# Attention over channels and a GELU layer in one kernel: the fifth chunk's squares of k folded, a copy of v moved to ScalarE, two fillers fewer, and a new order of steps up to block 6

## The chip, the cores and the metric

The kernel runs on one core of a Trainium2 chip. The metric is the time of one execution on the device in microseconds; here it is the median of three runs. A core has TensorE (matmuls, PE in the profile), VectorE (DVE), ScalarE (ACT), GpSimd (POOL), SyncE (SP) and 16 DMA engines. Each engine works through its own list in order.

## The reference

The inputs are q, k and v of shape (4, 6080, 256), w_in of (256, 2048) and w_out of (2048, 256), all in float32.

```python
qn = q / (np.linalg.norm(q, axis=1, keepdims=True) + 1e-06)
kn = k / (np.linalg.norm(k, axis=1, keepdims=True) + 1e-06)
s = kn.transpose(0, 2, 1) @ qn / tau            # 256 x 256 for each batch
a = np.exp(s - s.max(-1, keepdims=True))
a /= a.sum(-1, keepdims=True) + 1e-09
x = (v @ a).reshape(24320, 256)
h = x @ w_in
g = 0.5 * h * (1.0 + np.tanh(c * (h + 0.044715 * h * h * h)))   # c = sqrt(2 / pi)
out = g @ w_out
```

## The kernel before, in words

**Two halves for each batch.** For each of the four batches the kernel needs the Gram matrix G (q against k over 6080 rows) and the sums of squares of the columns of q and of k. From these come the scores and their exponentials (eT). Since v is only multiplied by a and then by w_in, the kernel builds aw, which is a times w_in (256 x 2048), once for each batch, and multiplies v's transposed rows (vT) by that. The rows of the output are worked in 25 blocks of about 1024 rows, each in two halves t=0 and t=1 of 512 rows. A block's first product is vT by aw with GELU on ScalarE, its second g by w_out. Parts of both go through seven instead of eight products of sub-blocks (lines 628 and 739), with the extra sums on VectorE.

**The first batch** cannot lie beside other blocks, so it is a stage of its own. Its rows come in six chunks (`FIRST`), 8 rows for each partition and 7 in the second. The first chunk is loaded in float32 and cast on chip; the others are cast by GpSimd's DMAs, the sixth in five pieces. For each chunk ScalarE squares q and VectorE squares k (line 172), side by side in one tile of 128 x 8 x 512. For the first four chunks `fold_first` (line 186) adds rows 0 to 3 and 4 to 7 of that tile, so that four rows are left. `gram_first` (line 199) does the Gram matmuls of a chunk. `ss_rows` sums squares over the partitions with matmuls against ones: for q one column at a time (line 217), for k one matmul of 256 columns for each row (line 223). On TensorE the sums of a chunk stand right ahead of the next chunk's Gram matmuls, and between the two `warm(n)` issues n matmuls of 256 columns whose result is not used (line 402). In the fifth and sixth chunk nothing is folded.

**From the sums to the first block.** Behind the last sums stand `warm(8)`, then `pe_vt(0, 0)`: TensorE's transposes of v's first half (line 337), then `scores` (lines 350 to 365: logarithms, exponentials and eT on ScalarE, S on VectorE), two copies of the transposed half out of PSUM on VectorE (`pe_vt_copy`, line 341), the load of the GELU table (line 886), and `first_aw`: row sums, their reciprocal rs (line 386) and the first 512 columns of aw, 256 of them copied by VectorE in four pieces (line 392) and 256 by ScalarE (line 395).

**The order of everything else** is a list written out by hand or by a planner beforehand (`ORDER`, 4017 steps), which the kernel walks through while it is built; the engines' lists follow it. A step is a block or batch and a short name:

- `0:j30` is the first product of block 0, 128 columns number 3, half 0 (line 560); `0:J30` its GELU (line 572).
- `0:s6m1` and the like are the products and sums of the seven-product scheme (lines 628 to 662).
- `b0:aw4` is a piece of aw for batch 0 on TensorE (line 501), `b0:ac4` its copy.
- `0:vp1` and `0:vc10` transpose a half of v on TensorE and copy it. Blocks 0 and 1 have three halves done so. The other halves are cast by a DMA of GpSimd (`1:lv1`, line 309) and transposed by a DMA of SyncE (`1:lt1`, line 321).
- `b1:lq0`, `b1:lk0` load a chunk of q or k of the next batch (line 246), `b1:r0.0` is a Gram row of it (line 296), `b1:zq0` its square on ScalarE, `b1:dk0` on VectorE, `b1:f0.1` a fold.
- `:pA11`, `:pF0` and others prepare the combinations of w_out.
- `0:T1a`, `0:M1A`, `0:c11`, `0:O0` are the sums, products, transposes and stores of the second half.

A load in the list waits for the matmul that stands last ahead of it (`GATE`). PSUM has eight accumulators, `FREE[1]`; one is taken from the front of the list and given back at its end.

**Buffers.** The pool `yout`, tag `ot`, has three buffers in rotation. In the first batch it holds the folded squares, then v's first halves as loaded for TensorE's transposes, later two tiles for w_out's sums and the output tiles:

```python
a1 = yout.tile([128, 4, 512], BF16, tag="ot", name=f"a1_{c}")
V0[m, t] = x = yout.tile([128, HALF // 128, C], BF16, tag="ot", name=f"v{m}_{t}")
```

Of the kernel before, what the change touches and what calls it, by code (L numbers as in the profile page):

```python
# [18 lines left out]
def kernel(  # L19
# [320 lines left out]
    def pe_vt_copy(m, t, cc):  # L340
        nc.vector.tensor_copy(vt(m)[:, t, cc, :], VPS[m, t][:, cc, :])
# [626 lines left out]
0:j01 0:j31 b0:w12 0:J80 0:s6ap 0:s6m7 0:s7m5 0:J61 :pA11 0:s6m3 0:J31 0:jb1 0:j41 b0:w01 0:J01
0:j90 0:ja0 :pF0 0:s6G1 0:s6ax 0:Jb1 0:s7y5 0:j71 0:M1A 0:Ja0 :pA12 b0:w03 0:J41 0:s6m4 0:J71 0:s7ap
:pF1 0:s6Gx 0:s7m7 b1:lk1 2:lv0 0:T3a 1:j50 0:M1B 0:J90 0:s7ax b1:lq2 0:s7m3 1:j01 b1:lk2 1:j10  # L970
0:s6Gr 1:J50 0:s7G1 b1:lk3 b1:r0.0 b1:r0.1 :pS2 0:s7m4 1:j51 1:j21 0:T1a 1:vs0 0:T2a 1:J01 1:j41
3:lv0 1:J10 0:x1 b1:dk0 b1:r0.2 b1:r0.3 8:lv0 b1:lq3 1:j31 1:J21 0:M2A 0:s7Gr 1:s3m1 b1:lk5 0:M2B
0:s7Gx b1:zq0 1:J31 :pS1 0:c11 0:T3b 0:M6A 1:s3cq b1:r1.0 1:j00 b1:r1.1 1:s3m5 1:vs1 1:J41 1:s3m2
0:T1b 1:J00 2:lv1 1:j11 b1:f0.1 0:M5A 1:J51 1:s3y5 b1:r1.2 1:s4m1 1:s3m6 1:s3ap 1:s3G0 b1:r1.3 1:j30
0:M5B 1:J11 b1:r2.0 :pNA 1:J30 1:s3m7 0:T2b 1:s4cq 4:lv0 1:s4m5 1:s4m2 0:y5 1:s4y5 1:s3m3 1:s3ax
1:vs2 1:s4m6 1:s4ap b1:zk1 1:s4G0 :pS4 b1:lq4 0:M6B 1:s3m4 b1:r2.1 1:s3G1 b1:r2.2 b1:r2.3 0:ap
b1:lk4 1:s5m5 b1:r3.0 1:s3Gx b1:zq1 1:s4m3 1:s4m7 1:j40 b1:r3.1 b1:lq5 1:s4ax 1:J40 0:M3A 1:s3Gr
b1:dk2 1:s4m4 b1:r3.2 1:s4G1 0:T4a 0:M3B b1:f1.1 1:s5m1 1:s6m1 1:s4Gx 1:s4Gr 1:s5cq 0:M7A 1:s5m2
1:s6cq 0:c12 1:s6m5 1:s5y5 1:s5G0 1:s5m6 0:T4b 0:M7B 1:s6m2 1:s6m6 1:j20 1:s6y5 1:s5ap 1:s5m7 2:lt1
b1:f1.2 b1:r3.3 1:s6ap b1:zq2 1:J20 b1:r4.0 1:s5ax 1:s6G0 b1:f2.1 1:s5m3 1:s6m3 2:lt0 1:s5G1 1:M1A  # L980
1:s7m1 1:s7m5 0:ax b1:r4.1 1:s6m7 1:s5m4 1:s5Gx 1:s6G1 b1:r4.2 1:s7y5 1:M1B 1:s7cq b1:zk3 1:s7m6
b1:f1.3 0:M4A 1:T3a 1:s5Gr 1:s6ax 1:s7ap 1:s6m4 1:s6Gx 1:s7m2 1:s7m7 b1:zq3 1:T1a 1:s7m3 b1:lk6
0:M4B 1:s7ax b1:f3.1 1:s6Gr 1:s7G0 b1:r4.3 1:s7G1 b1:lq6 2:j21 0:c21 2:j30 b1:lq7 b1:r5.0 1:x1 3:lv1
1:s7Gx 1:s7m4 2:J30 2:j20 2:j01 3:lt1 1:s7Gr 1:M2A b1:f3.2 2:j10 2:J21 2:J20 2:J01 2:s2m1 1:M2B
2:vs0 1:T3b 2:s2cq 2:J10 1:T1b 2:vs1 2:s2m5 2:j00 2:s2m6 2:s2y5 1:c11 2:vs2 2:s2m2 b1:dk4 2:s2ap
# [6 lines left out]
2:j31 2:s5m7 3:J31 2:s4Gx b1:dk6 2:s5ax 2:s6cq 2:s6y5 1:c22 1:O1 4:lv1 b1:lq8 b1:lk8 5:lv1 2:s5m3
2:J31 2:s5Gx 1:M4B 2:s6m2 2:s6m6 b1:r6.2 3:j21 b1:lk10 2:s5m4 1:c21 3:j10 b1:lq9 2:s6ap 2:s5G1
2:s7m1 3:J21 b1:r6.3 3:J10 2:s7cq 2:s6m3 2:T3a 2:s6m7 2:s7m5 b1:r7.0 2:s6G1 2:s6G0 b1:f5.2 b1:r7.1
2:s6ax b1:r7.2 2:s7m2 3:j11 2:s7m6 2:s6m4 2:s7y5 2:M1A 2:s5Gr 3:s2m1 3:J11 b1:f6.1 3:j01 2:s6Gx
2:s7ap 2:s6Gr 5:lv0 2:s7m7 b1:f5.3 2:s7m3 2:M1B 2:s7G0 3:j00 2:T1a 2:s7G1 b1:r7.3 2:s7ax 2:s7m4
3:J01 3:j20 2:x1 2:T2a 2:s7Gx 3:vs0 b1:zq7 b1:lq10 2:T3b 2:s7Gr 2:M2A 3:J00 3:J20 3:s2cq 2:M6A
b1:lq11 b1:f5.4 b1:lk9 b1:zk7 3:vs1 3:j30 2:M2B 3:s2m5 3:J30 3:s2m2 2:M5A 3:s2y5 2:T1b 2:c11 b1:lk11
2:M5B 2:T2b 3:s2G0 2:y5 3:s3m1 3:s2m6 b1:f7.1 3:s3cq 3:s2ap 3:vs2 2:M6B b1:zq9 3:s3m5 3:s3y5 2:ap
3:s3m6 3:s2m3 3:s2m7 b1:r8.0 3:s2G1 3:s3m2 2:M7A 3:s2ax 3:s2m4 2:M7B 3:s3ap b1:zq8 3:s4m1 3:s2Gr  # L1000
3:s3m3 3:s3G0 4:lt0 3:s4m5 b1:f7.2 b1:r8.1 2:M3A 3:s2Gx b1:r8.2 3:s4cq 3:s4m6 2:T4b 3:s4y5 2:ax 1:O0
2:T4a 3:s3G1 b1:zk9 3:s3m7 3:s4ap 3:s4m2 3:s4G0 3:s3ax 2:M3B 2:c12 3:s5m5 3:s3Gx 3:s4m7 3:s4m3 4:lt1
3:s3m4 b1:f7.3 3:s5m1 2:M4A 3:s4G1 2:M4B 3:s5cq 3:s3Gr 3:s5m2 3:s4ax 3:s6m1 3:s5m6 b1:dk8 3:s4Gx
b1:r8.3 b1:r9.0 3:s5y5 3:s5G0 2:c22 3:s6cq 3:s4m4 b1:r9.1 2:c21 5:lt0 3:s5ap 3:s6m5 3:s4Gr 3:s5m7
b1:f7.4 4:j30 3:s5m3 3:s6m2 3:s6y5 4:J30 b1:r9.2 b1:f8.1 3:s6G0 3:s7m1 b1:f9.1 3:s5ax b1:r9.3
b1:r10.0 b1:f9.2 3:s7cq 3:s6m6 3:s5G1 3:s7m5 2:O0 3:s7y5 b1:r10.1 b1:r10.2 3:s7m6 4:j00 b1:r10.3
3:s5Gx b1:r11.0 b1:zq11 b1:r11.1 3:s5m4 3:s6ap b1:r11.2 3:s7ap 3:s6m3 3:s7m7 3:s6m7 3:T3a 3:s5Gr
3:s7m3 5:lt1 3:s6ax 4:J00 3:s7m2 3:T1a 3:s7G1 4:j20 3:s6Gx 3:s6G1 4:j10 3:s7ax 3:s6m4 b1:dk10 3:s7G0
# [285 lines left out]
```

## Time and profile before

| what | value |
|---|---|
| median of three runs | 683.23 us (683.1 to 683.32) |
| the profiled execution | 683.62 us, its span 681.8 us |
| granted TensorE clock | 0.999 |
| busy: PE, DVE, ACT, POOL | 663.4, 626.1, 635.2, 87.8 us |
| bytes moved by DMA, mean rate | 78.80 MB, 116 GB/s |

Busy time is the time in which an engine had at least one instruction in work. Matmuls and ScalarE's steps overlap with their successors, so a step's duration is longer than its share: GELUs of 512 columns show a mean of 663 ns, and in a dense stretch (five in 2.55 us) follow each other at about 0.5 us. In the chain of waits a matmul of 512 columns has 0.215 us, and of 256 columns about 0.109. The time that an execution takes outside of its span is the difference of the first two figures in its row, 1.82 us.

### The profile page before, as it was taken

The numbers are of one execution on the slowest core, as the hardware profiler recorded it, in microseconds if no ns is written. First come the engines' busy times: TensorE is split into PE (matmuls) and PEld (weight loads), VectorE is DVE, ScalarE is ACT, GpSimd is POOL, SyncE is SP. The second block draws the span as 40 slices with busy tenths as digits, with TensorE's granted clock in tenths as the row PEclk, the third lists the DMA queues.
The fourth block names the chain that finished last, engine by engine and source line by source line (L and its number), as shares of the span: only waits on it lengthen the run. The fifth ranks groups of instructions, "written<-read, shape, count | busy, mean of one in ns | idle before, by whom it ended". The sixth has DMA issues, their size and how long they took to land.

```text
span 681.8 us, 10259 instructions
## 1 busy us (share of the span) xinstructions
PE 663.4 (97%) x3471; PEld 333.5 (49%) x3471; DVE 626.1 (92%) x922; ACT 635.2 (93%) x1224; POOL 87.8 (13%) x163
## 2 busy tenths in 40 slices
...
GB/s 241 208 258 157 122 139 163 140 87 129 79 137 81 136 163 131 141 68 120 115 136 43 158 98 147 126 117 78 62 68 106 75 67 122 39 55 78 83 31 121
DMA packets 165093, 78.80 MB, mean 116 GB/s; under 512 B 148992, under 2 KB 153472, under 8 KB 164320
## 3 DMA queue, kind: packets, MB, share of 16 engines
...
q10 hardware_dynamic: 1248, 1.28, 0.6%
q8 instruction: 27, 0.44, 0.3%
...
## 4 chain that ended last, share of the span: by engine, by line
PE 85%; DMA 6%; ACT 4%; DVE 3%; issue 1%; SPq 0%; POOL 0%; DVEq 0%; ACTq 0%; POOLq 0%
PE u L739 22%; PE rb L628 15%; PE j L560 13%; PE p L739 11%; PE qb L628 8%; PE c L739 5%; PE G L296 4%; PE qa L628 4%; DMA qk<-in_k_dram 3%; PE awp L501 2%; DMA out_dram<-ot 2%; DMA qk<-in_q_dram 1%; ACT sq L266 1%; ACT qa L643 1%; ACT g L572 1%
## 5 line engine op out<-in xcount | busy, mean ns | idle before, releaser
L739 PEld LDWEIGHTS <-wcomb 128*128 128x128 bf16 x1400 | 136.7, 98 | 146.2 <-issue 1.9
L739 PE MATMUL u<-t,wcomb 128*128 128x512 bf16 (+3 forms) x600 | 145.4, 368 | 0.0
L572 ACT ACTIVATE g<-j 128x512 bf16<-128x512 f32 (+1 forms) x204 | 127.0, 663 | 2.2 <-PE j L560 2.2
L560 PE MATMUL j<-vT,aw 128*128 128x512 bf16 (+2 forms) x456 | 126.6, 376 | 0.2 <-DVE aw L392 0.2
L648 DVE TENSOR_TENSOR qb<-rb,yw 128x512 f32<-128x512 f32 (+2 forms) x137 | 92.6, 680 | 9.9 <-PE rb L628 7.5
L628 PE MATMUL rb<-tv,sw 128*128 128x512 bf16 (+2 forms) x274 | 98.5, 374 | 0.0
L651 DVE TENSOR_TENSOR xw<-rb,yw 128x512 f32<-128x512 f32 (+2 forms) x137 | 91.8, 671 | 6.0 <-PE rb L628 3.5
L739 PE MATMUL p<-g,wcomb 128*128 128x512 bf16 (+3 forms) x400 | 96.4, 368 | 0.6 <-DVE g L712 0.5
L662 ACT ACTIVATE g<-xw 128x512 bf16<-128x512 f32 (+2 forms) x137 | 92.1, 675 | 1.3 <-DVE xw L651 1.3
L653 ACT ACTIVATE g<-qa 128x512 bf16<-128x512 f32 (+2 forms) x137 | 87.0, 640 | 2.8 <-PE qa L628 2.8
L656 ACT ACTIVATE g<-qb 128x512 bf16<-128x512 f32 (+2 forms) x137 | 87.6, 641 | 1.9 <-PE qb L628 1.6
L643 ACT ACTIVATE qa<-rb 128x512 f32<-128x512 f32 (+2 forms) x137 | 86.8, 638 | 1.7 <-PE rb L628 0.8
L646 ACT ACTIVATE yw<-qb 128x512 f32<-128x512 f32 (+2 forms) x137 | 87.1, 642 | 0.8 <-PE qb L628 0.5
L659 ACT ACTIVATE g<-rb 128x512 bf16<-128x512 f32 (+2 forms) x137 | 86.2, 640 | 1.4 <-PE rb L628 1.2
L628 PEld LDWEIGHTS <-sw 128*128 128x128 bf16 x548 | 53.6, 98 | 56.9 <-issue 1.9
L560 PEld LDWEIGHTS <-aw 128*128 128x128 bf16 x456 | 44.6, 98 | 45.2 <-DVE aw L392 0.7
L628 PEld LDWEIGHTS <-aw 128*128 128x128 bf16 x411 | 40.3, 98 | 42.3
L720 DVE TENSOR_TENSOR t<-g,g 128x2048 bf16<-128x2048 bf16 (+3 forms) x50 | 58.2, 1164 | 1.7 <-ACT g L662 0.8
L712 DVE TENSOR_TENSOR g<-g 128x2048 bf16<-128x2048 bf16 (+3 forms) x50 | 58.1, 1162 | 0.3
L718 DVE TENSOR_TENSOR t<-g,g 128x2048 bf16<-128x2048 bf16 (+3 forms) x50 | 57.8, 1160 | 0.1
L722 DVE TENSOR_TENSOR t<-t,g 128x2048 bf16<-128x2048 bf16 (+3 forms) x50 | 57.5, 1160 | 0.0
L309 POOL DMA_DIRECT2D vb<-in_v_dram x47 | 23.6, 503 | 222.1 <-PE rb L628 123.9
...
## 6 DMA issues: line engine op xcount, KB each, us to landing
...
wst<-in_moe_w_out_dram POOLq DMA_DIRECT2D x2, 1024.0 KB, 11.2
...
```

The source lines that it names most:

```text
L560: GATE[0] = nc.tensor.matmul(hp[:, :n].rearrange("p (t x) -> p t x", t=2) if t == 2 else hp[:, :n], lhsT=AW[b][:, cc, fc * 128 : fc * 128 ...
L572: nc.scalar.activation(g[:, t, fc % 8, :hc], hp[:, :hc], AF.Gelu_apprx_tanh)
L628: GATE[0] = nc.tensor.matmul(acc[:, :hc], lhsT=lhs, rhs=rhs, start=i in (1, 5), stop=True, skip_group_check=True)
L643: nc.scalar.activation(Q0[m, p][:, :hc], RB[m, p][:, :hc], AF.Copy)
L646: nc.scalar.activation(YW[m, p][:, :hc], Q1[m, p][:, :hc], AF.Copy)
L648: nc.vector.tensor_add(Q1[m, p][:, :hc], RB[m, p][:, :hc], YW[m, p][:, :hc])
L651: nc.vector.tensor_add(XW[m, p][:, :hc], RB[m, p][:, :hc], YW.pop((m, p))[:, :hc])
L653: nc.scalar.activation(g[:, 0, e, :hc], Q0.pop((m, p))[:, :hc], AF.Gelu_apprx_tanh)
L656: nc.scalar.activation(g[:, 1, e, :hc], Q1.pop((m, p))[:, :hc], AF.Gelu_apprx_tanh)
L659: nc.scalar.activation(g[:, 0, e + 1, :hc], RB.pop((m, p))[:, :hc], AF.Gelu_apprx_tanh)
L662: nc.scalar.activation(g[:, 1, e + 1, :hc], XW.pop((m, p))[:, :hc], AF.Gelu_apprx_tanh)
L739: GATE[0] = nc.tensor.matmul(ACCS[m, acc][:, :hc], lhsT=wcomb[:, w, fc, :], rhs=x[:, fc, :], start=first and k_ == 0, stop=k_ == 3, skip_g ...
```

## The change

In the first batch the squares of k of the fifth chunk (c = 4) are folded to four rows too, into a tile of the `ot` pool; the squares of q of that chunk stay as they are. `ss_rows` then takes four matmuls for k there instead of eight. Ahead of v's first transposes stand six fillers instead of eight. The second of the two copies of v's first transposed half is done by ScalarE. `square_later` can now take GpSimd as an engine, by steps `eq` and `ek`, but no step of the new list is one. The list `ORDER` holds the same 4017 steps; up to its 1099th, in block 6, they stand in another order, and behind that in the same.

```diff
+    SQK0 = {}
+
+    def fold_k(c):
+        a1 = yout.tile([128, 4, 512], BF16, tag="ot", name=f"a1_{c}")
+        nc.vector.tensor_add(a1[:, :, 256:512], SQ0[c][:, 0:4, 256:512], SQ0[c][:, 4:8, 256:512])
+        SQK0[c] = a1
...
     def ss_rows(c, which, rows=None):
         last = c == len(FIRST) - 1
-        n = N0.get(c, 8)
+        folded = which == 1 and c in SQK0
+        n = 4 if folded else N0.get(c, 8)
...
-        sq = SQ0[c]
+        sq = SQK0[c] if folded else SQ0[c]
...
     def pe_vt_copy(m, t, cc):
-        nc.vector.tensor_copy(vt(m)[:, t, cc, :], VPS[m, t][:, cc, :])
+        if (m, t, cc) == (0, 0, 1):
+            nc.scalar.copy(vt(m)[:, t, cc, :], VPS[m, t][:, cc, :])
+        else:
+            nc.vector.tensor_copy(vt(m)[:, t, cc, :], VPS[m, t][:, cc, :])
...
             if c < nch - 2:
                 fold_first(c)
+            else:
+                fold_k(c)
...
-        warm(8)
+        warm(6)
         pe_vt(0, 0)
         scores()
         pe_vt_copy(0, 0, 0)
```

The first steps of the list, before and after (cut):

```diff
-0:j00 b0:aw2 b0:aw3 0:j30 b0:ac2 0:J00 0:j10 b0:aw4 b0:ac3 b0:aw5 b0:aw6 0:J30 0:j20 0:J10 b1:lq1
-b0:w02 b0:w00 0:j60 b0:ac4 0:vp1 b0:ac6 0:s6m1 1:lv1 0:j40 0:J20 0:J60 b0:ac5 0:s7m1 0:s6cq 0:J40
...
+0:j00 0:j10 0:J10 b0:aw2 1:lv1 b0:aw3 b0:ac2 0:j20 b0:ac3 0:j30 b0:aw4 b0:w02 b0:aw5 b0:w00 0:j40
+0:J30 b0:ac4 b0:aw6 b0:ac5 0:j70 0:J20 1:lt1 0:vp1 b1:lq0 b0:ac6 0:vc10 0:J00 0:j80 0:J40 0:j60
+0:vc11 b0:w01 0:s6m1 0:J70 0:j90 0:vs0 0:J80 b0:aw7 0:jb1 0:s7m1 0:J60 0:s6cq b0:ac7 0:j81 0:vs1
+b1:lk0 0:j01 0:J90 b0:w10 0:Jb1 0:j11 0:s6m2 :pA11 0:s7cq 0:J81 0:J01 1:vp0 0:s7m2 b0:w12 b0:w03
+0:ja0 0:s6m5 b0:w11 1:vc00 0:J11 0:j51 0:s7G0 0:s6G0 0:j41 0:j21 0:s7m6 0:s6y5 0:vs2 0:J41 0:J51
...
```

More of the change, by code (lines that the diff above doesn't have):

```diff
@@ L251, with square_later @@
     SQ = {}
-    def square_later(b, c, which, on_act):
+    def square_later(b, c, which, on):
         n = chunk(c)[1]
@@ L968 @@
[L968 to L985, printed above, removed]
@@ L992 @@
[L992 to L1008, printed above, removed]
@@ L1019 @@
-4:s7G0 5:j01 4:s6G1 4:s7ap b1:krp 4:M1A 5:J01 4:s7m7 5:j00 b1:S0 5:j51 4:T3a 4:s5Gr 5:j50 4:s6Gx
-3:O1 b1:th0 4:s6m4 b1:S1 b1:th1 5:J00 4:s7ax 4:T1a b1:dn 4:s6Gr 5:j31 4:M1B b1:rc1 4:s7m4 4:s7m3
-5:J31 b1:rc3 b1:rc0 5:j41 b1:rc2 6:lt0 4:M5A 5:vs0 4:s7Gr 5:j21 5:J51 4:x1 5:j10 5:J50 4:s7G1 b1:eT
-5:J21 4:M2A 4:T2a 5:J41 5:s3m1 5:j30 5:s3cq 4:M2B b1:rsum 5:s3m2 5:J30 b1:aw6 5:J10 b1:rs 5:s3G0
-2:O1 4:s7Gx 5:vs1 b2:lq1 4:c11 5:j40 5:J40 b1:aw4 5:s3m5 4:M6A b1:ac6 5:s3m6 b1:aw2 5:s3y5 4:T3b
-b1:ac4 b1:aw3 5:vs2 5:s3ap b1:ac2 4:T1b b1:aw0 5:s3m3 5:s4m1 b1:aw7 b1:ac3 b1:w12 b1:ac0 5:s3m7
@@ new lines @@
+4:s6G0 4:s5Gx 3:c21 4:s5m4 b1:krp b1:S0 4:s5G1 b1:S1 4:s7m2 3:O1 4:T3a 4:s5Gr 4:s7G0 4:s6m7 4:s7m5
+5:j10 4:s6ax 5:j00 6:lt0 b1:th0 5:J10 4:M1A b1:th1 5:j51 4:s7y5 b1:dn 4:s7m6 4:T1a 4:M1B 4:s7ap
+5:J00 b1:rc2 4:s6Gx 4:s6m3 5:j30 4:s6m4 5:J51 4:s7m7 4:s6Gr 5:j50 4:s7ax 4:M5A 4:s7m4 5:J30 4:x1
+b1:rc3 b1:rc1 4:s7m3 4:s6G1 5:s3m1 4:s7Gr b1:rc0 5:J50 b1:eT 4:M2A 5:j01 5:j31 4:M2B 4:s7G1 5:vs0
+5:J01 b1:rsum 5:s3cq b1:aw6 5:J31 5:s3m2 5:vs1 b1:aw4 5:s3m6 b1:rs 4:s7Gx 5:j41 5:s3G0 5:s3m5 4:c11
+b2:lq1 b1:aw3 4:T2a b1:ac6 4:T3b b1:ac4 5:s3y5 5:j21 b1:aw2 5:J21 b1:w12 b1:ac2 5:s3ap 4:M6A b1:aw7
@@ new lines @@
+6:s5Gr 6:s6m7 6:s7G0 6:s7m5 6:s7y5 b2:r0.2 6:s6G1 7:j00 5:c22 6:s6ax 6:s7m6 b2:r0.3 6:j30 5:O1
+7:s2m1 b2:lq4 b2:r1.0 6:s7ap 10:lv0 6:s6Gx 6:J30 6:s7m3 6:s7m7 b2:lk5 6:s6m4 7:j11 6:s7G1 b2:r1.1
+7:s2cq b2:f2.1 6:s7ax 7:j10 7:J11 b2:f1.3 6:s7m4 b2:r1.2 6:s6Gr 6:s7Gr 7:s2m2 7:vs0 6:j00 7:j21
+b2:r1.3 9:lv0 7:vs1 7:s2m5 7:s2G0 b2:r2.0 b2:r2.1 6:J00 6:s7Gx 7:s3m1 7:s2y5 7:J21 6:T3a 6:T1a 7:J00
+b2:r2.2 6:M1A b2:r2.3 7:s2m6 7:s3cq 6:M1B 7:s3m2 b2:r3.0 b2:lq6 7:J10 6:x1 7:j31 7:s2ap 7:s2m3
+7:s3G0 b2:lq5 7:J31 7:s2m7 7:s3m6 7:s2G1 7:s3m5 7:vs2 6:M2A b2:lk4 7:s5m1 6:T3b 7:s2ax 6:T2a 7:s3y5
@@ new lines @@
+b2:r4.3 b2:r5.0 6:c22 7:s6m7 6:O1 b2:f3.4 7:s5Gr 7:s5Gx b2:lk7 b2:lq8 7:s7cq 7:s6m3 6:M4A 7:s6ax
+b2:r5.1 7:T3a 7:s7y5 b2:zk5 8:j00 7:s7m6 b2:lk8 9:lv1 7:s6G1 13:lv1 7:s6Gx 6:M4B 8:j11 7:s7ap 6:c21
+8:J00 7:s7m7 7:s6m4 7:s7m3 8:J11 8:j20 7:s7ax 7:s7m2 8:j30 7:s6Gr 7:s7m4 b2:r5.2 8:J20 8:j10 7:s7G0
+7:T1a 7:M1A 7:s7G1 10:lv1 8:J30 b2:lq7 8:vs0 7:s7Gr 8:s2m1 8:J10 7:s7Gx 8:j21 8:s2cq 7:M1B b2:f5.1
+8:s2m5 7:T2a 8:j01 8:J21 7:x1 8:s2m2 8:vs1 b2:f4.1 7:T3b 8:J01 7:T1b 8:s2m6 8:s2y5 8:s2G0 b2:r5.3
+b2:r6.0 8:s2ap 8:vs2 8:s3m1 7:M2A 8:s3m5 8:s3cq b2:r6.1 b2:r6.2 7:T2b 7:M2B 8:s3m2 8:s2m3 8:s3y5
@@ new lines @@
+10:j20 9:s6m1 b2:r11.2 b2:f11.1 9:s4Gr 9:s5m7 10:J20 9:s5m3 9:s7m1 10:lt1 9:s6cq 8:c22 b2:f11.2
+9:s5G1 9:s6m5 9:s6y5 9:s7cq b2:r11.3 9:s6m6 b2:gc 8:M4A 9:s6m2 9:s5ax 8:M4B 9:s7m5 9:s6ap 9:s6G0
+10:j00 b2:f11.3 9:s7m2 b2:f11.4 9:s5Gx 9:s6m7 8:c21 9:s7y5 9:s6m3 10:J00 9:s7m6 b2:ss 9:s6ax 10:s2m1
+9:s5m4 9:s7G0 9:s7ap 9:s6G1 9:s6Gx 9:s6m4 9:s7m7 10:s2cq 9:s7m3 9:T3a 9:s6Gr 9:M1A 10:s3m1 b2:sv
+9:s7ax 9:s7G1 b2:pow 10:j01 10:s2m2 9:T1a 9:s5Gr 9:s7m4 10:s3cq 10:J01 10:j30 9:M1B 10:j10 10:vs0
+10:J30 9:M5A 9:s7Gx 9:s7Gr 10:vs1 b2:kf 10:vs2 10:s3m6 10:J10 9:T3b 10:s2m6 9:T2a 9:T1b 9:x1 10:s3m2
@@ new lines @@
+10:s5G0 10:s5ap 10:s6cq 10:s4m3 9:ax 11:j00 11:J31 10:s5m7 10:s5m3 11:J00 10:s5ax 10:s4G1 10:s6m5
+10:s6y5 b3:lk0 10:s6m2 10:s6m6 10:s7m1 10:s5m4 10:s6G0 10:s5G1 9:M4A b2:rc0 10:s5Gx 11:j01 10:s6ap
+10:s7m5 10:s7cq b2:rc1 10:s6m7 9:M4B 10:s6ax 10:s7m6 11:J01 10:s7y5 10:s6m4 b2:rc2 10:s7m2 10:s7G0
+10:M1A 10:s7ap 10:s5Gr 10:s6Gx b2:eT 10:s6m3 11:j10 10:s7m3 10:s7m7 11:J10 10:M1B b2:aw5 12:lt1
+9:c21 10:s7ax 10:T3a 10:s7m4 b2:rsum 11:vs0 10:s7G1 10:s6Gr 10:s6G1 10:x1 10:s7Gr b2:aw7 11:j30
+b2:aw3 11:J30 10:M2A 10:s7Gx b2:rs b2:aw1 10:T1a 9:c22 b2:ac5 b2:ac3 b2:ac1 10:T3b 11:s2m1 b2:aw2
@@ new lines @@
+11:J11 11:s5y5 11:s4ap 10:T4a 11:s5cq 11:s4m7 11:s4m3 11:s4G1 11:s4ax b3:lq1 b2:w02 11:s4Gx 10:M3B
+11:s4m4 11:s4Gr 11:s5m6 11:s6cq 11:s5m2 11:s5ap 10:c12 10:M7B 11:s6m5 11:s5G0 11:s5m3 10:ax 11:s6m6
+11:s5m7 11:s6y5 11:s6m2 11:s5G1 12:j10 10:M4A 11:s6G0 11:s7m5 11:s5ax 11:s5Gx 11:s6ap 11:s7m1 12:J10
+b2:w11 11:s7cq 11:s5m4 11:s6m3 11:s6m7 10:M4B 11:T3a 12:j30 11:s7m6 11:s6ax 11:s7y5 11:s6m4 11:s6G1
+10:c21 12:j00 10:O0 12:j31 11:s7ap 11:s5Gr 11:s6Gx 11:s7m3 11:s7m7 10:c22 11:s6Gr 12:j21 12:J30
@@ new lines @@
+b3:lk3 12:s7G0 13:j01 12:s6ax b3:r1.1 12:s5Gr 12:s6m4 12:J11 13:j00 13:J01 12:s6Gx 12:s7ap b3:lq6
+12:s7m7 b3:lk5 13:j20 b3:r1.2 12:T3a 12:s7ax 13:J00 12:s7m3 b3:r1.3 12:s6Gr 13:J20 13:j10 12:T1a
+12:s6G1 13:J10 13:s2m1 b3:lk4 12:s7m4 12:s7Gr 14:lv0 12:s7Gx 15:lv0 12:M1A 13:s2cq 13:vs0 b3:dk2
+13:vs1 b3:r2.0 13:j11 b3:lq5 13:j21 12:T2a b3:r2.1 12:M1B b3:r2.2 13:vs2 13:s2m5 12:s7G1 13:J21
+13:J11 13:s3m1 13:s2m6 13:s2m2 12:x1 13:s2y5 12:T3b b3:zq2 b3:r2.3 11:c22 12:T1b 13:j31 b3:lq4
+13:s2G0 12:M2A 13:s2ap 12:M2B 12:c11 12:M6A b3:zk3 b3:f1.3 13:s3cq 13:s2m7 12:T2b 13:J31 12:M5A
```

509 lines of the change are left out of this document (253 added, 256 removed).

## The prediction

> **What bounds the kernel now.** First the page's busy rows and chain, to see which engine carries the span:
>
> ```profile
> span 681.8 us, 10259 instructions
> PE 663.4 (97%) x3471; PEld 333.5 (49%) x3471; DVE 626.1 (92%) x922; ACT 635.2 (93%) x1224; POOL 87.8 (13%) x163
> PE 85%; DMA 6%; ACT 4%; DVE 3%; issue 1%; SPq 0%; POOL 0%; DVEq 0%; ACTq 0%; POOLq 0%
> ```
>
> TensorE is the bound, with ScalarE and VectorE close behind. Then the busy time by stretches of 10 us, for where TensorE still has holes:
>
> ```profile
> 30.00:40.00 10.00, 9.77 (x109) 7.33 (x107) 6.22 (x15) 6.43 (x12) 5.43 (x7) 1.00 1.31 202
> 40.00:50.00 10.00, 10.00 (x59) 5.01 (x58) 8.86 (x20) 8.92 (x19) 2.17 (x4) 1.00 1.12 304
> 50.00:60.00 10.00, 10.00 (x52) 4.96 (x51) 9.73 (x14) 10.00 (x21) 3.13 (x6) 1.00 0.76 119
> ```
>
> From 40 us TensorE has no hole; it stays at 10.00 in every such stretch up to 300. ScalarE has 1.1 us free between 40 and 50 and nothing after 50. So in the body, where most of the diff lies, the old order leaves nothing to win on TensorE: another order of the same steps can tie or lose. What can be won lies ahead of 37.6 us. There the chain of waits (start, length, what) and the timeline say what ends last:
>
> ```profile
> 11.47 17.19 DMA qk<-in_k_dram
> 28.70 1.91 PE G L199 x16
> 30.61 0.87 PE ss L223 x8
> ...
> 34.88 0.90 PE warm L402 x8
> 35.77 0.46 PE vt_ps L337 x8
> ```
>
> ```profile
> 31.51 2.00 DVE L182 TENSOR_TENSOR sq<-qk 128x1280 bf16<-128x1280 bf16 x3 [1.61 <-DMA qk<-in_k_dram]
> 34.92 0.26 ACT L355 ACTIVATE lnq<-ss,eps 128x2 f32<-128x2 f32 x1
> 35.54 0.91 ACT L365 ACTIVATE eT<-S,rq 128x256 bf16<-128x256 f32 x2
> 36.26 0.76 DVE L341 COPY vT<-vt_ps 128x512 bf16<-128x512 bf16 x2 [0.59 <-PE vt_ps L337]
> 36.47 1.28 ACT L886 ACT_TABLE_LOAD   x1
> 36.93 0.16 DVE L386 RECIPROCAL rs<-sums 128x2 f32<-128x2 f32 x1
> 37.62 0.65 PE L560 MATMUL j<-vT,aw 128*128 128x512 bf16 x2 [0.23 <-DVE aw L392]
> ```
>
> Chunk 4 of k lands at 28.7, then TensorE runs without a hole to about 36; the softmax (lnq, rq, eT), rs and the aw copies lead to the first product j at 37.62. That start moves everything behind it.
>
> **The change, part by part.** Sums are made against the profiled execution (683.62 us: span 681.8 and 1.82 around it), which is 0.39 above the median of 683.23.
>
> *Fold of chunk 4.* VectorE gets one addition of 128x1024 in bf16; the nearest row, a<-sq at L276, takes 0.68. It starts after the square (28.68 + 1.23) and ends at 30.6; VectorE was idle 1.61 us there, so it costs VectorE nothing. TensorE would stand at ss L223 at 30.44, so it waits 0.15, then does 4 matmuls instead of 8: eight took 0.87 in the chain, so 0.44 is saved. Net 0.29, but the next matmuls need the first piece of k of chunk 5, and VectorE's wait for it ended at 31.51; they started at 31.72. So 0.19 to 0.2 is left up to the end of the sums (34.54 instead of 34.74). The last pieces of q landed at 33.82, early enough. lnq, rq and eT follow: eT 35.34, TensorE's sums for it at 35.9 instead of 36.1. If the fold came late, its cover gone, at most the 0.44 is given back and the stage stands as before.
>
> *The fold's tile* turns the three-buffer pool of output tiles by one. The load of v's first half now waits for the sums of chunk 2 (they ended at 23.33) instead of chunk 1; it issued at 23.43 anyway and landed 11.7 us later, at 35.13, behind other loads in GpSimd's queue. Cost nothing; a later issue by some tenths is hidden by those 11.7 us.
>
> *Two fillers fewer.* 0.22 less ahead of v's transposes: they start at 35.2 instead of 35.6. v's landing (35.13) just allows it. They were not last (eT was), so no gain by itself.
>
> *The copy on ScalarE.* VectorE's two copies (36.26, 0.76 together) held rs back: sums ended at 36.70, rs came at 36.93. With one copy, rs follows its sums at 36.55, 0.38 earlier, and j starts at 37.24. On ScalarE the copy stands ahead of the table load. No row shows a ScalarE copy of 16-bit PSUM; bounds are VectorE's own 0.42 and the 0.76 of the aw copies at L512. I take 0.5, as ScalarE's steps of this width are 0.48 apart. Its first GELU then comes at 38.8 to 38.9, after 38.49 before. Behind that copy are queued the table, two aw copies and all GELUs; their waiters have 0.51 us of idle before the second GELU as cover.
>
> *The first steps of the order.* j10 now follows j00 at once and needs the later two of the four aw copies (1.13 together): ready at 37.96, so TensorE waits 0.2 to 0.3. When the first two aw products are done, at 39.05, it has issued 8 matmuls; before it had 6 at 38.96. Two are 0.43, so it is 0.34 ahead.
>
> *The rest of the new order* (a quarter of the list, to block 6, near 204 us; equal behind that) holds the same 3206 matmuls from j00 on. Gain: none. Loss: ScalarE has 0.5 us more to do and starts later. From j30's GELU to j41's are 19 steps of 0.485, 9.2 us, with 0.4 of waits between them; TensorE has 9.7 us of matmuls until it needs the bank that j41 frees. So they meet there, at 50 us, and for six accumulators in a row each pair of matmuls (0.43) waits for a ScalarE step (0.48): 6 x 0.05 = 0.3. Bounds: 0 (the 1.1 us free between 40 and 50 hold) and 0.8 (the copy and the later start in full). I take 0.3.
>
> *Loads that are moved.* On GpSimd's queue the cast of block 1's v is moved up, ahead of the first loads of batch 1; it lands behind the second w_out half (48.66) at about 49.9, and its transposing DMA 4.0 later (the duration of before) at 53.9; its first reader comes at 54.1 to 54.4. For block 2 the first reader of the two transposing DMAs follows their gate by 16 matmuls of 512 and 6 of 256 columns, 4.1 us; before by 6.9 and 6.5. They took 3.1 to 3.4 when issued alone, 4.5 to 4.7 as the close pair they were there; now they are 3.6 apart. I take no stall, bound 0.7 each. k of chunk 1 of batch 1 has 5.8 us instead of 7.4 and took 4.1. SyncE's queue holds only these and stores.
>
> Sum: -0.34 + 0.3 = -0.04; 683.58 against the profiled execution, 683.2 against the median.
>
> *A rule weighed.* TensorE was slow in its first matmuls (421 ns for 256 columns, later 273), and 1.0 us of idle at 27.7 did not bring that back. The change adds idle of 0.1 to 0.3 at a time. The Trainium skill, "TensorE: Matmul & The Clock Gate", Part 1, has the clock halved after an idle window of about 3.4 us; by that, too, fewer fillers cost nothing here, whereas its warning of oscillation by frequent micro-idles is the clock rival below.
>
> **The rivals.** *ScalarE does not pace (faster, but small).* For it: the 1.1 us free. Then -0.34, with up to 0.3 more if the copy is cheap: 682.6 to 682.9. *Late transposing DMAs (slower).* Block 2's both take 4.5 to 4.7 as in the old pair, decided by landing over 3.9 us: 2 x 0.7 = 1.4, and 0.2 for block 1's: 684.8. For it: 16 DMA engines over 0.7 busy there; against it: lone ones at 3.4 even at 1.01. *The clock falls near 36 us (slower).* At the early 421 against 273 ns, three us of matmuls take 1.6 more: 684.8; against it the granted clock of 1.00 throughout. *A stall disappears (faster).* VectorE idles 1.89 us at 417 for a store that took 12.6 behind a burst of seven loads; if the shift breaks that up, -1.9: 681.3. Against it: order and gates there are unchanged. *The fold does nothing*, as it waits and k's landing follows: +0.2 on my sum, inside the forecast.
>
> **How the numbers follow.** Forecast (nothing net, 682.9 to 683.8): 0.56. No pacing: 0.16. Late DMAs: 0.18. Clock or another new wait of over 1.4 us: 0.06. The stall gone: 0.04. What a measurement of this kernel can tell from no change is about 0.2%, 1.4 us: faster 0.04, same 0.56 + 0.16 = 0.72, slower 0.24. The range from 682.6 to 684.8 takes in the first two cases and most of the third.
>
> **What would show it.** Right: L223 in chunk 4 with 4 matmuls, G at 31.5, eT near 35.3, rs near 36.55, j at 37.2; TensorE at 10.00 from 40 on with tenths lost near 50 to ScalarE's GELUs; block 6 reached within 0.5 us of before. Wrong: v landing after 35.2, a copy on ScalarE of a us or more, TensorE waiting for vT in blocks 1 or 2, a stretch before 205 us under 9.8, or a granted clock under 1.

## The result and the profile after

| | before | after |
|---|---|---|
| median beside each other | 683.28 us (682.76 to 683.93, 6 runs) | 687.73 us (685.99 to 690.55, 6 runs) |
| the profiled execution | 683.62 us, span 681.8 | 690.55 us, span 688.8 |
| granted TensorE clock in it | 0.999 | 0.995 |

The changed kernel is slower: the ratio is 1.0068, with an interval from 1.0047 to 1.009. The forecast was 683.2 us with a range up to 684.8, so it was wrong, and on the wrong side. The runs of the changed kernel also spread over 4.6 us, those of before over 1.2. The profiled execution is the longest of the six, so what it shows is the full size of a loss that other runs have in part: the shortest run, 685.99, had a granted clock of 1.000.

The page shows where the extra time is. These are its span, its busy row, the chain's shares by engine, and the group of the first products (busy and mean ns, then idle time ahead of them and what ended it):

```profile
span 688.8 us, 10250 instructions
...
PE 667.3 (97%) x3465; PEld 334.1 (49%) x3465; DVE 626.3 (91%) x922; ACT 636.0 (92%) x1225; POOL 88.2 (13%) x163
...
PE 82%; DMA 8%; ACT 4%; DVE 4%; issue 1%; SPq 0%; POOL 0%; DVEq 0%; ACTq 0%; POOLq 0%
...
L571 PE MATMUL j<-vT,aw 128*128 128x512 bf16 (+2 forms) x456 | 129.1, 379 | 4.0 <-DMA vT<-vb 3.9
```

DMA's share of the chain rose from 6 to 8%. TensorE waits 3.9 us in all for a transposed half of v (vT<-vb), and it is busy 3.9 us longer (667.3 against 663.4) with six matmuls fewer, which means that some of its matmuls took longer. The busy time by stretches of 10 us, which answers to the second view of the prediction (stretch, its length, PE, PEld, DVE, ACT, POOL, then granted clock, DMA share, GB/s), says when:

```profile
30.00:40.00 10.00, 9.70 (x105) 6.93 (x103) 6.37 (x16) 6.61 (x12) 5.95 (x8) 1.00 1.30 201
40.00:50.00 10.00, 10.00 (x59) 5.01 (x58) 9.81 (x21) 9.19 (x19) 1.37 (x2) 1.00 1.12 304
50.00:60.00 10.00, 6.43 (x26) 2.50 (x25) 5.96 (x8) 6.80 (x13) 1.05 (x2) 0.89 1.01 98
60.00:70.00 10.00, 10.00 (x43) 4.58 (x41) 6.84 (x10) 6.92 (x13) 3.15 (x6) 0.77 0.65 90
```

Up to 50 us nothing is lost. Between 50 and 60 TensorE is busy for 6.43 us where it had 10.00, and between 50 and 70 the granted clock is 0.89 and 0.77 where it had 1.00. From the chain of waits (start, length, what):

```profile
48.42 1.29 PE j L571 x6
49.71 0.26 PE rb L639 x2
49.98 8.55 DMA vT<-vb
58.52 0.05 issue
58.57 1.03 PE j L571 x2
```

The transposing DMA of block 1's v is issued at 49.98 and lands 8.5 us later. Before, it was issued at 51.05, took 4.0 and landed at 55.05, ahead of its first reader at 56.5. In the new order the last matmul ahead of the reader ended at 55.0, and TensorE stood until 58.57, 3.56 us. The same busy times, cut finer, show what follows from that idle time:

```profile
54.00:57.00 3.00, 1.00 (x5) 0.27 (x3) 2.88 (x3) 2.80 (x5) 0.53 (x1) 1.00 1.27 66
57.00:58.00 1.00, 0.00 (x0) 0.00 (x0) 0.00 (x0) 0.00 (x0) 0.00 (x0) 0.86 1.05 183
58.00:61.00 3.00, 2.43 (x6) 0.87 (x7) 0.86 (x2) 0.08 (x1) 0.53 (x1) 0.50 0.41 76
61.00:64.00 3.00, 3.00 (x10) 1.32 (x9) 2.70 (x3) 2.87 (x6) 0.53 (x1) 0.50 0.82 107
64.00:65.00 1.00, 1.00 (x6) 0.49 (x5) 0.00 (x0) 0.23 (x1) 0.00 (x0) 0.72 0.88 164
65.00:68.00 3.00, 3.00 (x18) 1.55 (x16) 1.63 (x3) 1.74 (x4) 1.05 (x2) 1.00 0.55 70
```

At about 57.7 us, still within the wait, the granted clock falls to 0.50 and stays there until about 64.6 (0.86 in the slice from 57 and 0.72 in the slice from 64 are mixtures of 1.00 and 0.50). From 58.57 to there TensorE works 6.0 us at half clock, which by estimate loses half of that, 3.0. The wait and this are 6.5 of the 6.9 us by which the profiled execution is longer (690.55 against 683.62); the other 0.4 is the size of a second, short wait for a transposed half in block 2 (0.36).

What occupied the DMA engines meanwhile is in the queues and issues between 49.5 and 59 us (packets, MB, share of 16 engines; then the issues with us to landing), here of the changed kernel:

```profile
q1 hardware_dynamic: 1056, 0.26, 57.4%
...
q<-in_q_dram POOLq DMA_DIRECT2D x1, 256.0 KB, 7.9
...
vT<-vb SPq DMA_TRANSPOSE x1, 8.5
```

and the same two rows of the kernel before:

```profile
q1 hardware_dynamic: 1056, 0.26, 16.3%
...
vT<-vb SPq DMA_TRANSPOSE x1, 4.0
```

The same 1056 packets of the transposing DMA took 57.4% of the engines' time in place of 16.3%, 3.5 times as much, while the engines together moved less (110 against 126 GB/s in that stretch). In the new order the load `b1:lq1` of q is issued 0.46 behind the transposing DMA (start, us on the issuing queue):

```profile
49.98 1.34 SPq L329 DMA_TRANSPOSE vT<-vb  x1
50.44 0.53 POOL L254 DMA_DIRECT2D q<-in_q_dram  x1 [3.31 <-PE rb L639]
```

In the old one a load of q was issued 1.88 ahead of it, and none for 4 us behind it:

```profile
49.17 0.54 POOL L246 DMA_DIRECT2D q<-in_q_dram  x1 [2.48 <-PE j L560]
51.05 1.32 SPq L321 DMA_TRANSPOSE vT<-vb  x1
```

The list alone does not show this neighbourhood. The step `1:lt1` stands 56 steps ahead of `b1:lq1`, but its DMA starts only when the cast of v has landed, here at 49.9. That difference in order was the first suspect.

### The profile page after: what moved, and what is told of

It reads as the page before. It is cut to its first block, busy times and chain, and to the rows that moved or that the text cites. A ratio compares the mean times of both kernels' runs of the same rounds, so it can differ in the third digit from the quotient of the medians.

```text
span 688.8 us, 10250 instructions
## 1 busy us (share of the span) xinstructions
PE 667.3 (97%) x3465; PEld 334.1 (49%) x3465; DVE 626.3 (91%) x922; ACT 636.0 (92%) x1225; POOL 88.2 (13%) x163
## 4 chain that ended last, share of the span: by engine, by line
PE 82%; DMA 8%; ACT 4%; DVE 4%; issue 1%; SPq 0%; POOL 0%; DVEq 0%; ACTq 0%; POOLq 0%
PE u L750 21%; PE rb L639 15%; PE j L571 12%; PE p L750 11%; PE qb L639 7%; PE c L750 5%; PE qa L639 4%; PE G L304 4%; DMA qk<-in_k_dram 3%; PE awp L512 2%; DMA vT<-vb 2%; DMA out_dram<-ot 2%; DMA qk<-in_q_dram 1%; ACT sq L274 1%; ACT qa L654 1%
## 5 line engine op out<-in xcount | busy, mean ns | idle before, releaser
L571 PE MATMUL j<-vT,aw 128*128 128x512 bf16 (+2 forms) x456 | 129.1, 379 | 4.0 <-DMA vT<-vb 3.9
L583 ACT ACTIVATE g<-j 128x512 bf16<-128x512 f32 (+1 forms) x204 | 122.7, 641 | 7.8 <-PE j L571 7.7
L659 DVE TENSOR_TENSOR qb<-rb,yw 128x512 f32<-128x512 f32 (+2 forms) x137 | 92.5, 679 | 10.3 <-PE rb L639 6.9
L673 ACT ACTIVATE g<-xw 128x512 bf16<-128x512 f32 (+2 forms) x137 | 90.2, 661 | 1.4 <-DVE xw L662 1.3
L664 ACT ACTIVATE g<-qa 128x512 bf16<-128x512 f32 (+2 forms) x137 | 85.5, 630 | 2.9 <-PE qa L639 2.8
L667 ACT ACTIVATE g<-qb 128x512 bf16<-128x512 f32 (+2 forms) x137 | 85.9, 628 | 2.3 <-PE qb L639 1.9
L654 ACT ACTIVATE qa<-rb 128x512 f32<-128x512 f32 (+2 forms) x137 | 85.4, 627 | 2.0 <-PE rb L639 0.8
L657 ACT ACTIVATE yw<-qb 128x512 f32<-128x512 f32 (+2 forms) x137 | 85.5, 630 | 0.8 <-PE qb L639 0.5
L670 ACT ACTIVATE g<-rb 128x512 bf16<-128x512 f32 (+2 forms) x137 | 84.5, 626 | 1.2 <-PE rb L639 1.1
L639 PEld LDWEIGHTS <-sw 128*128 128x128 bf16 x548 | 53.9, 98 | 58.0 <-issue 2.4
L571 PEld LDWEIGHTS <-aw 128*128 128x128 bf16 x456 | 44.6, 98 | 49.5 <-DMA vT<-vb 4.7
L304 PE MATMUL G<-k,q 128*128 128x256 bf16 (+1 forms) x288 | 51.2, 275 | 0.0
```

The lines of the kernel that those rows point to most:

```text
L571: GATE[0] = nc.tensor.matmul(hp[:, :n].rearrange("p (t x) -> p t x", t=2) if t == 2 else hp[:, :n], lhsT=AW[b][:, cc, fc * 128 : fc * 128 ...
L583: nc.scalar.activation(g[:, t, fc % 8, :hc], hp[:, :hc], AF.Gelu_apprx_tanh)
L639: GATE[0] = nc.tensor.matmul(acc[:, :hc], lhsT=lhs, rhs=rhs, start=i in (1, 5), stop=True, skip_group_check=True)
L654: nc.scalar.activation(Q0[m, p][:, :hc], RB[m, p][:, :hc], AF.Copy)
L657: nc.scalar.activation(YW[m, p][:, :hc], Q1[m, p][:, :hc], AF.Copy)
L659: nc.vector.tensor_add(Q1[m, p][:, :hc], RB[m, p][:, :hc], YW[m, p][:, :hc])
```

## The experiments

Theory A: what is lost is the wait for block 1's transposed half, and the half clock behind it; the DMA is long because the load is issued right behind it. Rival B: the head's edits (fold, fillers, copy on ScalarE) cost it. Rival C: the new order loses in many small waits. Later a rival D was added: the DMA is long because of the new order's other traffic, whatever the load's place. Each kernel below ran beside the kernel before on the same chip; the median of before was 683.39 for four of them (head's edits, new order, reader later, load later), 683.5 for the next four (both cures, load earlier, load behind in the old order, 26 fillers) and 683.72 for the last two. The diffs of the list are cut to the steps that move.

**The head's edits with the old order.** The list `ORDER` is that of before, all else as changed.

```diff
-0:j00 0:j10 0:J10 b0:aw2 1:lv1 b0:aw3 b0:ac2 0:j20 b0:ac3 0:j30 b0:aw4 b0:w02 b0:aw5 b0:w00 0:j40
...
+0:j00 b0:aw2 b0:aw3 0:j30 b0:ac2 0:J00 0:j10 b0:aw4 b0:ac3 b0:aw5 b0:aw6 0:J30 0:j20 0:J10 b1:lq1
...
```

> The three edits of the head (fold of chunk 4, six fillers, the copy on ScalarE) with the old order of steps. Theory A (the loss is the wait for block 1's transposed half of v in the new order, and the slow clock behind that wait): the head edits cost nothing; 0.1 to 0.4 us are won, 682.9 to 683.2; block 1's transposing DMA takes about 4.0 us as before and nobody waits for it. Rival B (the head edits cost: ScalarE's copy delays its GELUs): 684 or more, with ScalarE as the releaser of TensorE's waits near 50 us.

Measured: 683.02 us (682.51 to 683.96), ratio 0.9996 with an interval from 0.9987 to 1.0004. The transposing DMA took 3.8 us, a load standing 1.88 ahead of it. B falls: the head's edits cost nothing, and their gain, 0.4 us by the medians, is not told from none.

**The new order with the old head.** The reverse: the functions of before, the list of after.

```diff
-            else:
-                fold_k(c)
...
-        warm(6)
+        warm(8)
...
```

> The new order of steps with the old head (eight fillers, chunk 4 unfolded, both copies on VectorE). Theory A: the whole loss stays, 685.5 to 690, with a wait of 2 to 5 us of TensorE for vT near 55 us. Rival B: the loss goes, 683 to 684.

Measured: 687.48 us (685.26 to 688.75), ratio 1.0056 [1.0037, 1.0076]. So the list alone carries the loss. In the profiled execution (686.36) the DMA took 7.7 us, with the load 0.76 behind it, and TensorE's wait between 50 and 62 us was (in all, times, longest):

```profile
PE j L560 <- DMA vT<-vb: 2.4, 1, 2.4
```

The granted clock stayed at 1.00 through this shorter wait. The execution was 3.0 longer than the median of before, 683.39; waits for transposed halves are 2.6 of it over its whole span, and 0.3 is lost at 50 us to ScalarE's pace, which the section on the prediction comes back to.

**The reader put later.** In the changed kernel the products of block 1's half 1 (the half that comes by DMA) change places with those of half 0 (which TensorE transposed).

```diff
-b1:lk1 0:T3a 1:j31 0:s7m7 b1:lk2 1:j21 0:s7ax :pA12 0:s6G1 0:s6m4 1:J21
+b1:lk1 0:T3a 1:j30 0:s7m7 b1:lk2 1:j20 0:s7ax :pA12 0:s6G1 0:s6m4 1:J20
...
```

> The changed kernel, but in the list the columns 2 and 3 of block 1's first product change their halves: 1:j31 and 1:j21 become 1:j30 and 1:j20 and the other way round, GELUs too, so that the first reader of the transposed half stands some 4 us of matmuls later. Theory A: nearly the whole loss goes, 682.5 to 684, the granted clock stays at 1.00 near 60 us. Rival C (the new order loses in many small waits): 685 or more.

Measured: 683.84 us (682.53 to 684.29), ratio 1.0003 [0.9994, 1.0011]. The DMA still took 6.8 us (the load came 0.18 behind it), but nobody waited for it, and the granted clock was 1.00 from 50 to 70. The whole loss is gone with the wait, so C falls: no crowd of small waits is left that could be told from nothing.

**The load put later.** `b1:lq1` stands behind `1:j00` in place of behind `0:Ja0`.

```diff
-0:s6m6 0:Ja0 b1:lq1 0:J21 0:ja1
+0:s6m6 0:Ja0 0:J21 0:ja1
...
-0:s6m3 1:j00 0:s7ap
+0:s6m3 1:j00 b1:lq1 0:s7ap
```

> The changed kernel, with one load (b1:lq1, 256 KB of q) moved from just ahead of block 1's transposing DMA to behind 1:j00, 4 us later. If the transposing DMA took 8.5 us because it shared the DMA engines with this load, it takes 3 to 4.5 us now and the time is 683 to 684. If its length has another cause, it still takes 6 to 9 us and the time is 686 to 690.

Measured: 683.62 us (683.07 to 684.28), ratio 1.0004 [0.9995, 1.0013]. The issues between 45 and 56 us (start, us on the issuing queue):

```profile
46.24 0.80 POOL L254 DMA_DIRECT2D k<-in_k_dram  x1 [2.90 <-PE j L571]
49.89 1.35 SPq L329 DMA_TRANSPOSE vT<-vb  x1
55.22 0.53 POOL L254 DMA_DIRECT2D q<-in_q_dram  x1 [8.18 <-PE j L571]
```

With the load at 55.22 the DMA took 3.5 us. One load in another place, and the loss is gone.

**Both cures together.** The reader later and the load later.

```diff
-b1:lk1 0:T3a 1:j31 0:s7m7 b1:lk2 1:j21 0:s7ax
+b1:lk1 0:T3a 1:j30 0:s7m7 b1:lk2 1:j20 0:s7ax
...
-0:s6m3 1:j00 0:s7ap
+0:s6m3 1:j00 b1:lq1 0:s7ap
...
```

> The changed kernel with both cures: the products of block 1's half 1 stand behind those of half 0 (1:j31, 1:j21 swapped with 1:j30, 1:j20), and the load b1:lq1 stands behind 1:j00. If the wait and the half clock behind it are all that the new order costs, the two cures add nothing to each other: 683.0 to 683.8 us, a transposing DMA of 3.5 to 4.2 us, no TensorE wait for it, granted clock 1.00 from 50 to 70 us. If the head's 0.3 us were being hidden by the 0.2 us wait that was left with the moved load, 682.9 to 683.3. If the swap or the move costs something of its own: over 684.

Measured: 683.86 us (682.5 to 684.55), 0.06 above the first range expected, ratio 1.0004 [0.9995, 1.0013]; the DMA took 3.5, and nobody waited for it. The cures add nothing to each other. None of these kernels is shown to beat the kernel before: the new order without its wait stands 0.2 to 0.5 above before by the medians of four kernels, the head alone 0.4 below, and each of their intervals holds 1.

**The load put earlier.** In the changed kernel `b1:lq1` stands ahead of `0:ja0`, about as far ahead of the transposing DMA as a load stood in the old order.

```diff
-:pA11 0:s7cq 0:J81 0:J01 1:vp0 0:s7m2 b0:w12 b0:w03 0:ja0
+:pA11 0:s7cq 0:J81 0:J01 1:vp0 0:s7m2 b0:w12 b0:w03 b1:lq1 0:ja0
...
```

> The changed kernel with the load b1:lq1 moved ahead of 0:ja0, so that it is issued some 2 us ahead of the transposing DMA of block 1's v (near 47.7 us) and not 0.5 behind it. The old order had a load 1.9 ahead of it and the DMA took 4.0. If what lengthens the DMA is a load that is issued right behind it, it takes 3.5 to 4.5 and lands by 54.5, no wait of over 0.5, 683.2 to 684.2. If it is any load that shares the engines with it, it takes over 6 and the loss stays: 686 to 689.

Measured: 683.81 us (682.98 to 684.71), ratio 1.0004 [0.9995, 1.0013]. The issues:

```profile
47.73 0.53 POOL L254 DMA_DIRECT2D q<-in_q_dram  x1 [0.94 <-PE qa L639]
49.91 1.33 SPq L329 DMA_TRANSPOSE vT<-vb  x1
```

With the same load 2.18 ahead of it, the DMA took 4.7 (0.2 more than was expected at most), and no matmul waited for it. The load's bytes are the same; its place decides. D falls here, and from the other side in the next.

**A load behind the DMA in the old order.** In the kernel before, the load `b1:lk1` moves up behind `0:s7m5`.

```diff
-0:s6ap 0:s6m7 0:s7m5 0:J61 :pA11
+0:s6ap 0:s6m7 0:s7m5 b1:lk1 0:J61 :pA11
...
-0:s7m7 b1:lk1 2:lv0
+0:s7m7 2:lv0
```

> The kernel before, with one load (k of chunk 1 of batch 1, b1:lk1) moved up to be issued near 51.5 us, some 0.4 behind the transposing DMA of block 1's v. If a load issued right behind it is what lengthens that DMA, it takes 6.5 to 8.5 in place of 4.0, lands at 57.6 to 59.6, and its first reader (56.5) waits 1.1 to 3: 684.4 to 687, more if the clock falls. If the length belongs to the new order's other traffic, it stays near 4.0 and the time at 683.3 within 0.6.

Measured: 687.89 us (685.39 to 689.42), ratio 1.0058 [1.0036, 1.0081]. The issues, and TensorE's wait between 50 and 62:

```profile
48.88 0.54 POOL L246 DMA_DIRECT2D q<-in_q_dram  x1 [2.48 <-PE j L560]
50.80 1.34 SPq L321 DMA_TRANSPOSE vT<-vb  x1
51.47 0.53 POOL L246 DMA_DIRECT2D k<-in_k_dram  x1 [2.06 <-PE qb L628]
```

```profile
PE j L560 <- DMA vT<-vb: 2.2, 1, 2.2
```

The DMA took 7.8 in place of 4.0. One load moved in the kernel before makes the whole loss; the median was even 0.9 above what was expected, as two of the four runs, 688.92 and 689.42, had a granted clock of 0.996 and 0.994.

**Two loads behind the DMA.** In the changed kernel `b1:lk1` follows `b1:lq1` at once.

```diff
-0:s6m6 0:Ja0 b1:lq1 0:J21
+0:s6m6 0:Ja0 b1:lq1 b1:lk1 0:J21
...
```

> The changed kernel with a second load (b1:lk1, 256 KB) put right behind b1:lq1, so that two loads are issued within 1.1 us behind the transposing DMA of block 1's v. If every load issued right behind it lengthens it by the engines' time that it takes, the DMA takes 10 to 13 us, TensorE waits 5 to 8, and since every wait is then over 3.5 the clock falls in every run: mean clock 0.996 or less, 691 to 696 us. If the first load alone does it (the second is queued behind the first), 7 to 8.5 us and 686 to 690.6, as the changed kernel.

Measured: 691.21 us (689.33 to 692.46), ratio 1.0104 [1.0081, 1.0127]. The DMA took 10.3, the wait was 5.4, and the busy times show the half clock again:

```profile
57.00:58.00 1.00, 0.00 (x0) 0.00 (x0) 0.00 (x0) 0.00 (x0) 0.00 (x0) 0.82 0.91 138
58.00:61.00 3.00, 0.88 (x3) 0.33 (x4) 0.00 (x0) 0.00 (x0) 0.00 (x0) 0.50 0.50 90
61.00:64.00 3.00, 3.00 (x9) 1.07 (x8) 2.31 (x3) 1.53 (x4) 1.06 (x2) 0.50 0.30 28
64.00:67.00 3.00, 2.95 (x17) 1.69 (x17) 2.11 (x4) 1.65 (x4) 0.53 (x1) 0.92 0.87 142
```

A second load makes the DMA some 2 to 3.5 us longer than one did (6.8 to 8.5). A mean clock of 0.996 or less was expected in every run; two of four had 0.997 and 0.998, so that half missed.

**Fillers in the wait.** To part the wait from the clock, the changed kernel gets fillers into the accumulator of `1:j31` ahead of its own products.

```diff
         HP[m, fc, t, 1], _ = hp, _ = take(("j", m, fc, t), 1, [128, 512], f"j{m}_{fc}_{t}", width=n)
+        if (m, fc, t) == (1, 3, 1):
+            for _ in range(26):
+                nc.tensor.matmul(hp[:, :256], lhsT=ones_bf, rhs=zeros_bf, start=True, stop=True, skip_group_check=True)
```

> The changed kernel with 26 filler matmuls of 256 columns (some 2.8 us of TensorE) written into the accumulator of 1:j31 ahead of its own products: they fill the wait for block 1's transposed half, and no result changes. If the half clock follows from the idle wait, the granted clock stays 1.00 from 57 to 65 us and the time is before plus the larger of the wait and 2.8: 686.1 to 687.0, the mean clock 1.00 in every run, and less spread between runs than the 686.0 to 690.6 of the changed kernel. If the half clock has another cause (a limit of power, or the moment), it comes again: 688 to 691 with a clock of 0.50 for some us. If the wait costs little and the clock nearly all, the fillers cost 2.8 in place of 3 to 4: hardly told apart from the first.

Measured: 686.21 us (685.34 to 686.49), ratio 1.0035 [1.0021, 1.0049]. The DMA was as long as ever, 7.8 us, and the clock stayed:

```profile
54.00:57.00 3.00, 3.00 (x27) 2.41 (x25) 2.57 (x3) 2.50 (x5) 0.53 (x1) 1.00 1.21 127
57.00:58.00 1.00, 0.95 (x7) 0.57 (x7) 0.00 (x0) 0.00 (x0) 0.00 (x0) 1.00 1.07 193
58.00:61.00 3.00, 3.00 (x18) 1.62 (x18) 2.56 (x4) 2.20 (x5) 1.05 (x2) 1.00 0.40 46
```

The fillers do nothing useful, and yet the kernel is 1.5 us faster than the changed one by the medians (on another chip, where before was 0.2 slower), with a spread of 1.2 over four runs in place of 4.6 over six. The fillers themselves take 3.0 in the trace, so what this kernel loses against before, 2.7 (686.21 less 683.5), is the most that the wait can cost by the medians. Of the median loss of 4.4 (687.73 less 683.28) some 1.7 is left for the half clock that follows the wait in some executions. This split is an estimate, as the mean clock does not name those executions: 6.8 us at half clock take 0.005 off it, which 690.55 (0.995) and 687.45 (0.996) show, but 688.66 had 0.998, as some runs of before had too (so had 688.6 and 688.75 of the new order with the old head). Whether their waits were longer or their half clock shorter stays open.

**Half the fillers.** The same with `range(12)`.

```diff
-            for _ in range(26):
+            for _ in range(12):
```

> The changed kernel with 12 filler matmuls of 256 columns (some 1.3 us) in place of 26 ahead of the products of 1:j31. The wait stays 2.5 to 3.9 in all, but the unbroken idle behind the fillers is only 1.2 to 2.6. If the unbroken idle sets the half clock, the clock stays 1.00 from 57 to 65 us and the time is 685.5 to 687.0, as with 26. If the time without real work sets it, the clock falls as in the changed kernel in some runs: 686 to 690.6, with a mean clock of 0.996 or less there.

Measured: 686.41 us (684.04 to 688.51), ratio 1.0039 [1.0026, 1.0053]. In the profiled execution the DMA took 6.9, 0.63 us of idle was left behind the fillers, and the clock was 1.00. Eight of ten runs lay at 686.62 or below, two of these (684.04 and 684.82) under the range expected; two, 688.36 and 688.51, lay some 1.4 above what was expected without a fall of the clock. Their mean clock was 0.998, and of them there is no trace, so whether their wait was longer or their clock fell stays open.

Side by side, the transposing DMA of block 1 in all these profiles:

| loads issued near it | kernels | us to landing |
|---|---|---|
| none from 3.6 ahead to 5.2 behind | load later; both cures | 3.5, 3.5 |
| one, 1.9 to 2.2 ahead | before; head only; load earlier | 4.0, 3.8, 4.7 |
| one, 0.2 to 0.8 behind | after; new order; reader later; fillers; half the fillers | 8.5, 7.7, 6.8, 7.8, 6.9 |
| one 1.9 ahead and one 0.7 behind | load behind in the old order | 7.8 |
| two, 0.4 and 0.9 behind | two loads | 10.3 |

These edits, one of a single load in each order, show that the load's place sets the length. Why a load behind costs so much more than a load ahead is not shown; each figure is from one execution.

## Why the prediction was wrong, point by point

**The step that failed: loads that are moved.** The prediction gave block 1's cast 49.9 us and its transposing DMA "4.0 later (the duration of before)". The first was right (the DMA was issued at 49.98). The duration was carried over from an execution in which no load stood behind the DMA into an order that puts one there. With 8.5 in place of 4.0 it lands at 58.5, not 53.9. The reader was placed at 54.1 to 54.4; without the wait it would have started at about 54.8 (0.43 behind the two products that start at 54.41), 0.9 behind the landing that was forecast, where before it started 1.4 behind the landing (56.48 less 55.05). That margin was the quantity to guard. The bound of 0.7 came from other transposing DMAs of the trace (3.1 to 4.7), but none in that trace had a load issued within 3.9 us behind it: the rows could not show the case, and the bound was too narrow for that reason.

**The rival of late transposing DMAs** named the mechanism and put it in the wrong block. It gave block 2 1.4 us and block 1 only 0.2; block 2's wait measured 0.36 in the changed kernel and up to 0.6 in the others traced, block 1's 2.2 to 3.6 with one load behind. Its price of 684.8 was short by 1.4 of what the wait alone brings (686.21 with the fillers), and its chance, 0.18, was too low. Its argument against, that lone DMAs took 3.4 even with the engines' share at 1.01, took the mean share for the cause; the place of the load is one.

**The clock rival** priced the half clock at 1.6 us, which the 1.7 by the medians happen to meet and the 3.0 of the profiled execution do not, and it had the wrong place. It was argued at 36 us, as a matter of its own, with a chance of 0.06 that it shared with other waits. It is no independent case: it hangs on a long wait (3.56 us brought it, 2.4 did not), and belonged into the price of the late DMA.

**The rule weighed.** Idle of 0.1 to 0.3 at a time cost nothing in the head, as forecast. The other side of the rule was not used: the Trainium skill, "TensorE: Matmul & The Clock Gate", Part 1, halves the clock after an idle window of about 3.4 us. The traces agree in kind: waits of 2.2 and 2.4 us left the clock at 1.00, waits of 3.56 and 5.4 halved it. They differ in one number: the granted clock fell at 57.7 and 57.6, about 2.7 and 2.9 us after TensorE's last matmul had ended (55.0 and 54.7), less than the page's window.

**The fold of chunk 4** did what was said, with a smaller net gain. The timeline of the changed kernel:

```profile
30.22 0.69 DVE L194 TENSOR_TENSOR a<-sq 128x1024 bf16<-128x1024 bf16 x1
...
30.97 0.60 PE L231 MATMUL ss<-a,ones_bf 128*128 128x256 bf16 x4
...
36.58 0.59 ACT L350 COPY vT<-vt_ps 128x512 bf16<-128x512 bf16 x1
...
36.83 0.17 DVE L397 RECIPROCAL rs<-sums 128x2 f32<-128x2 f32 x1 [0.28 <-PE sums L394]
...
37.51 1.16 PE L571 MATMUL j<-vT,aw 128*128 128x512 bf16 x4
```

The addition took 0.69 (0.68 taken) and four matmuls stand at L231. Chunk 4 landed 0.2 later in this execution (its Gram matmuls began at 28.91, not 28.70), which has to be taken off each time below. The sums came at 30.97; without a wait they would have come 1.74 after the start of the Gram matmuls, as before, at 30.65, so TensorE waited 0.3 in place of 0.15: the prediction's sum had left out the gaps between the square's end, the addition and the sums (0.10 and 0.06). eT came at 35.62, 35.4 with the landing's 0.2 taken off, against 35.54 before: 0.1 gained, not 0.2.

**The copy on ScalarE** took 0.59, within its bounds of 0.42 and 0.76 and above the 0.5 taken. With one copy less on VectorE, rs followed its sums at once, as forecast. j began at 37.51, 37.3 with the landing's 0.2 taken off; 37.24 was forecast. **The fold's tile** and **the two fillers** cost nothing, as forecast: v's load was issued 0.9 later and nobody waited for it.

**ScalarE's pacing**, 0.3 at 50 us, came in its place and size. Five pairs of first products follow each other there, before and after:

```profile
51.51 2.32 PE L560 MATMUL j<-vT,aw 128*128 128x512 bf16 x10
...
50.02 2.55 PE L571 MATMUL j<-vT,aw 128*128 128x512 bf16 x10
```

The pairs start 0.49 apart after and 0.43 before, and with the product behind them some 0.3 is lost. ScalarE's eight GELUs of that stretch take 4.08, so they follow each other at 0.50; the profile names no releaser for the pairs, so that ScalarE holds them is argued from the equal pace. Every traced kernel with the new order has the 2.55, the one with the old head too, so the extra copy on ScalarE is not its cause. A stretch of 10.00 busy hides such a loss, since a matmul's record is longer than its share.

Without the long wait, the forecast's two terms hold: some 0.3 won in the head, 0.3 lost at 50 us. The four kernels with the new order and without that wait stand 0.2 to 0.5 above before, which this measurement does not tell from none. Three of them show a short wait in block 2 (0.2, 0.4 and 0.6), where none was taken.
